# Giving one batch's softplus, half-splitting and transpose copies first place on their engines

## The chip, the cores and the metric

The kernel runs on one core of a Trainium2 chip. The metric is the time of the whole program on the device, in microseconds, as the median of several runs. The core has five engines that work side by side, each through a list of instructions of its own: TensorE (PE, matmuls; the loading of their weights is listed apart as PEld), VectorE (DVE), ScalarE (ACT), GpSimd (POOL) and SyncE (SP), which here issues the DMA transfers.

## The reference: what is computed

```python
def sm_attn(qq, kk, vv):                       # per batch and head
    s = scale * np.matmul(qq, kk.transpose(0, 1, 3, 2))
    s = s - np.max(s, axis=-1, keepdims=True)
    a = np.exp(s)
    a = a / (np.sum(a, axis=-1, keepdims=True) + 1e-09)
    return np.matmul(a, vv)
p_packed = sm_attn(p, k, v)                    # 32 packed queries look at 576 tokens
out = sm_attn(q, p_packed, p_packed)           # 576 tokens look at the 32 packed rows
...
x = out.transpose(0, 2, 1, 3).reshape(B * S, H * D)
h = x @ w_in
g = np.maximum(h, 0.0) + np.log1p(np.exp(-np.abs(h)))      # softplus
return g @ w_out
```

There are 8 batches of 576 tokens, 8 heads of 64, and a feed-forward part of 512 to 2048 to 512. q, k, v and p are float32; w_in and w_out arrive as 64-bit floats, and the kernel turns them into 32-bit ones itself.

## The kernel before: how the work is staged

**Algebra.** For one batch the second attention gives weights `aT` (packed rows by tokens, in two groups of four heads) that multiply `p_packed`. The kernel never forms `out`: it multiplies `p_packed` by `w_in` first (`make_m`, result `m`), and then `h = m^T @ aT`. Products that need more precision than one pass gives are made from a high and a low half of both sides, three matmuls instead of four: `at_h`/`at_l` (lines 525 and 526), `mh`/`ml` (558 and 559), `gh`/`gl` (594 and 595), `wo_h`/`wo_l` (238 and 244). The high half is a copy on ACT (or DVE for `gh`), the low half is the difference, made on DVE.

**Units.** After the attention of batch 0, the main loop goes through 128 units, a unit being one batch b and one block f of 128 columns of the 2048. Unit (b, f) has `gemm1` (line 580: twelve matmuls into two banks `ph` of 288 tokens), then softplus: ACT takes the absolute value of both banks (602), the exponential (604) and the logarithm (605), DVE then takes the maximum with 0 of `ph` and adds (607), which is the last reader of the banks. Two banks `ph` exist, so the next unit's `gemm1` waits for this. For batch 0 the exponential and the logarithm go over all 576 tokens at once, in other batches bank by bank. POOL sets the last 64 tokens aside (611), DVE splits the others into `gh` and `gl`. Two units later `gemm2` (618) multiplies them by `wo_h` and `wo_l`: four blocks of tokens, three matmuls each, accumulated over f in four banks `acc`. Units 0 and 1 of batch 0 have no `gemm2` beside them yet.

**Between the units.** At unit u, `make_m` for unit u + 2 is issued when a new group of columns begins. In batch 0 such a group has 256 columns, so that it comes at every second unit; in the others it has 512. It takes two banks out of the pool `ps_m`, which has two, and the same two banks serve each small product of the attention of the next batch, which is spread in steps between the blocks of `gemm2`.

**Turned q and k.** For batches 0 and 1, `transposed` (lines 254 to 269) turns q and k by matmuls with an identity into a bank (262), and ACT copies the bank to SBUF (268, `T_k` and `T_q`). For later batches DVE turns them (254). During batch 0's units the attention of batch 1 runs, so its sixteen copies `T_k` and `T_q` fall there; those of batch 0 come before the first unit.

**Conversion of the weights.** `convert` is a generator over 32 tiles, sixteen of w_in and sixteen of w_out, in the order i0 i1 o0 o1 i2 i3 o2 o3 and so on. One tile takes a load by SP (156), two steps of ACT (200 and 204, which make `m` and `r`), two of DVE (206 and 211) and one addition of POOL (219), which writes `w_in_sb` directly or, for w_out, a tile `t` from which ACT makes `wo_h` and DVE `wo_l`. Two to four staging tiles take turns: from the seventeenth tile on there are two. The steps begin in the attention of batch 0 and go on through its units, 1.6 steps after each block of `gemm2`. A tile of w_in is needed by `make_m`, a tile of w_out by `gemm2`.

**What sets the order.** PE's instructions stand in the order in which the text issues them (`manual_schedule` for PE alone). Those of the other engines are ordered when the program is built: of the operations that are ready by the builder's own reckoning, the one with the highest priority is taken, and without further word the one issued earlier in the text has the higher one. `tc.high_priority(offset=FRONT)`, FRONT being 1000, moves what is issued inside it ahead by that much. In the kernel before, the steps of batch 0's attention, `make_m(0, 0)` and `weights(0)` stand in it. On the chip each engine goes through its list in the order thus fixed.

Of the kernel before, what the change touches and what calls it, by code (L numbers as in the profile page):

```python
# [2 lines left out]

# [23 lines left out]
def pack_attention_then_softplus_ffn(  # L27
# [10 lines left out]
    nc = tc.nc  # L38
# [7 lines left out]
    C = S // 2  # L46
# [40 lines left out]
    def bank(nm):  # L87
        if spare:
            spare.append(spare.pop(0))
            pool, tag = spare[-1]  # L90
            return pool.tile([P, 512], F32, tag=tag, name=nm)
        return ps_m.tile([P, 512], F32, tag="m", name=nm)
# [164 lines left out]
    def transposed(nm, b, g, hh):  # L257

        src = loaded[nm, b, g]
        ps = bank(f"psT_{nm}_{b}_{g}_{hh}")  # L260
        for i in range(HS):
            nc.tensor.transpose(
                ps[:, i * NP:(i + 1) * NP],
                src[:, hh, 2 * i:2 * i + 2, :].rearrange("x s d -> x (s d)"),
                ident[:NP, :NP],
            )
        dst = work.tile([P, C], F32, tag="T", name=f"T_{nm}_{b}_{g}_{hh}", bufs=4)
        nc.scalar.copy(dst, ps[:, :C])  # L268
        return dst

    def scores(nm, b, g, c, lhs, rhs):
# [259 lines left out]
    def m_cols(b):  # L531

        return MC if b else MC // 2

    def make_m(b, c, res):


        n = m_cols(b)
        pss = [bank(f"psm_{b}_{c}_{g}") for g in range(G)]
        for g, ps in enumerate(pss):  # L540
            for hh in range(HG):
                o = D * g
                nc.tensor.matmul(  # L543
                    ps[hh * J:(hh + 1) * J, :n],
                    res["pt"][g][o:o + D, hh * J:(hh + 1) * J],
                    w_in_sb[o:o + D, hh, c * n:(c + 1) * n],
                    start=True, stop=True,
                )
        pool, th, tl = (cv, "t", "r") if b and c % 2 == 0 else (work, "mh", "ml")
        halves = []  # L550
        for g, ps in enumerate(pss):
            o = g * n % MC
            if o == 0:
                mh = pool.tile([P, MC], F32R, tag=th, name=f"mh_{b}_{c}_{g}", bufs=2)
                ml = pool.tile([P, MC], F32R, tag=tl, name=f"ml_{b}_{c}_{g}", bufs=2)
                halves.append((mh, ml))
            cols = slice(o, o + n)
            nc.scalar.copy(mh[:, cols], ps[:, :n])  # L558
            nc.vector.tensor_tensor(  # L559
                ml[:, cols], ps[:, :n], mh[:, cols].bitcast(F32), op=ALU.subtract  # L560
            )
        res["m"][c] = halves
# [112 lines left out]
    FRONT = 1000  # L675
# [15 lines left out]
    res = [{"pt": [], "aT": {}, "m": {}} for _ in range(B)]  # L691
# [24 lines left out]
    ahead, chain, due = iter(()), iter(()), 0.0  # L716
    for u in range(len(units) + LAG):
        if u < len(units):
            b, f = units[u]
            if f == 0:  # L720
                if (b + 1) % BG == 0 and b + 1 < B:
                    pack_transposed((b + 1) // BG, pt)
                ahead = attention(b + 1) if b + 1 < B else iter(())
                due = 0.0
            chain = softplus(b, f, gemm1(b, f, res[b]), gs)
            next(chain)
            if f == NF - 1:
                if (b + 2) % BG == 0 and b + 2 < B:
                    pt = load_pack((b + 2) // BG, (nc.sync,))
                for _ in ahead:  # L730
                    pass
                if b + 1 < B:
                    weights(b + 1)
        if u >= LAG:
            b2, f2 = units[u - LAG]
            gh, gl = gs.pop((b2, f2))
            if f2 == 0:
                acc = [ps_acc.tile([P, DM], F32, tag="acc", name=f"acc_{b2}_{t}") for t in range(NT)]
        last = u >= LAG and f2 == NF - 1 and b2 % 2 == 1
        if last:  # L740
            both = rests(b2)
            next(both)
        for t in range(NT):
            if u >= LAG:
                gemm2_tile(
                    acc[t], gh, gl, f2, slice(t * P, (t + 1) * P), f2 == 0, f2 == NF - 1
                )
                if f2 == NF - 1:
                    store(acc[t], [(0, b2, t * P, P)], f"{b2}_{t}", t)
            if u < len(units):  # L750
                due += PACE if b != FIRST - 1 else PACE_FIRST
                while due >= 1:
                    next(ahead, None)
                    due -= 1
                if b == 0:
                    cdue += CONV
                    while cdue >= 1:
                        next(conv, None)
                        cdue -= 1
            next(chain, None)  # L760
        if last:
            next(both)
        if u + 2 < len(units):


            nb, c = units[u + 2][0], units[u + 2][1] * P
            if c % m_cols(nb) == 0:
                make_m(nb, c // m_cols(nb), res[nb])


# [27 lines left out]
```

## Time and profile before

| | us |
|---|---|
| median of 3 runs | 775.51 |
| lowest and highest of them | 773.61 and 777.2 |
| the profiled execution | 774.48 |
| its span, first to last instruction | 772.7 |

The profile is of one execution, taken by the hardware profiler. Times are microseconds from the start of the span. A row of the timeline has start, length, engine, line of the kernel, operation, output and inputs, and in brackets how long the engine was idle before it and which operation ended this. A row of the waits has the waiting engine and line, the one it waited for, and the sum, the number and the longest of the waits. A row by stretch has the stretch, its length, the busy time of PE, PEld, DVE, ACT and POOL with the number of instructions, the granted clock of PE as a share of full speed, the share of the DMA engines and GB/s. Over the whole span PE is busy 94%, DVE 68%, ACT 56% and POOL 13%.

### The profile page before, as it was taken

How to read it: one execution, taken by the hardware profiler on the slowest of the kernel's cores; microseconds unless marked ns; L12 is line 12 of the kernel's file. 1: busy time of each engine (PE TensorE's matmuls, PEld its weight loads, DVE VectorE, ACT ScalarE, POOL GpSimd, SP SyncE). 2: the span in 40 equal slices, each digit the busy share in tenths (PEclk: the TensorE clock that was granted, in tenths of full speed). 3: DMA queues.
4: the chain of work that ended last, by engine and by line, in shares of the span. 5: the costliest groups of instructions: out<-in, count | busy, mean ns of one | idle time of the engine just before them, and what ended most of it. 6: DMA issues, size and time to landing. Idle time of an engine off the chain costs nothing.

```text
span 772.7 us, 14153 instructions
## 1 busy us (share of the span) xinstructions
PE 729.3 (94%) x5360; PEld 577.0 (75%) x5360; DVE 527.4 (68%) x1092; ACT 435.3 (56%) x1057; POOL 99.0 (13%) x166
## 2 busy tenths in 40 slices
PE   6457997999999999999999999999999999999997
PEld 4346675687788778877887777878787777888886
DVE  2697869975877559575877559576877558565554
ACT  5667977666455445565555455565555355555540
POOL 1253434200000000000010000000010000000110
PEclk9969999999999999999999999999999999999999
DMA  9977644534302342052402332043401400010002
GB/s 205 247 194 179 180 133 125 120 74 78 76 17 68 63 68 57 1 116 47 87 0 69 62 63 62 1 98 51 92 1 55 75 2 1 1 55 1 1 1 68
DMA packets 149668, 55.97 MB, mean 72 GB/s; under 512 B 116320, under 2 KB 142944, under 8 KB 149600
## 3 DMA queue, kind: packets, MB, share of 16 engines
q1 hardware_dynamic: 149328, 55.00, 31.9%
q8 instruction: 42, 0.69, 0.4%
q14 instruction: 26, 0.21, 0.1%
q10 hardware_dynamic: 272, 0.07, 0.0%
HBM read 45.61 MB, written 9.44 MB: 71 GB/s over the span
## 4 chain that ended last, share of the span: by engine, by line
PE 82%; DVE 6%; ACT 6%; DMA 4%; POOL 1%; issue 1%; SPq 0%; ACTq 0%; DVEq 0%; POOLq 0%
PE acc L618 41%; PE ph L580 26%; PE acc_m L618 6%; PE psm L543 4%; PE ps L275 2%; DMA w_in_sb<-in_q 2%; PE psp L318 1%; PE psa L308 1%; DMA k<-in_k 1%; ACT m L200 1%; DVE at_l L526 1%; DVE t L211 1%; POOL t L219 1%; ACT e L604 1%; DVE t L206 1%
## 5 line engine op out<-in xcount | busy, mean ns | idle before, releaser
L602 ACT ACTIVATE e<-ph 128x288 f32<-128x288 f32 x256 | 103.1, 404 | 189.3 <-PE ph L580 142.4
L618 PE MATMUL acc<-wo_h,gh 128*128 128x512 f32 x512 | 207.6, 405 | 0.0
L607 DVE SCALAR_TENSOR_TENSOR e<-ph,e 128x288 f32<-128x288 f32 x256 | 113.3, 451 | 131.9 <-ACT e L605 128.2
L618 PE MATMUL acc<-wo_l,gh 128*128 128x512 f32 x512 | 200.9, 392 | 0.0
L618 PE MATMUL acc<-wo_h,gl 128*128 128x512 f32 x512 | 200.8, 392 | 0.0
L580 PE MATMUL ph<-at_h,mh 128*128 128x288 f32 x512 | 158.9, 310 | 14.8 <-ACT at_h L525 7.5
L580 PE MATMUL ph<-at_l,mh 128*128 128x288 f32 x512 | 153.3, 299 | 3.7 <-DVE at_l L526 3.7
L580 PE MATMUL ph<-at_h,ml 128*128 128x288 f32 x512 | 152.7, 298 | 0.0
L580 PEld LDWEIGHTS ph<-at_h,mh 128*128 128x128 f32 x512 | 97.6, 191 | 48.8 <-DVE e L607 10.8
L611 POOL COPY rest<-e 128x64 f32<-128x64 f32 x128 | 53.2, 416 | 575.8 <-DVE e L607 544.2
L618 PEld LDWEIGHTS acc<-wo_h,gh 128*128 128x128 f32 x512 | 96.2, 188 | 27.4 <-issue 10.2
L618 PEld LDWEIGHTS acc<-wo_h,gl 128*128 128x128 f32 x512 | 96.1, 188 | 21.0
L604 ACT ACTIVATE e<-e 128x288 f32<-128x288 f32 (+1 forms) x240 | 109.5, 456 | 3.9
L605 ACT ACTIVATE e<-e 128x288 f32<-128x288 f32 (+1 forms) x240 | 109.4, 456 | 3.2
L618 PEld LDWEIGHTS acc<-wo_l,gh 128*128 128x128 f32 x512 | 96.4, 188 | 13.0
L580 PEld LDWEIGHTS ph<-at_l,mh 128*128 128x128 f32 x512 | 97.8, 191 | 8.2 <-DVE at_l L526 5.3
L580 PEld LDWEIGHTS ph<-at_h,ml 128*128 128x128 f32 x512 | 97.8, 191 | 0.0
L595 DVE TENSOR_TENSOR gl<-e,gh 128x512 fp32r<-128x512 f32 x128 | 87.7, 685 | 5.5
L558 ACT CAST mh<-psm 128x512 fp32r<-128x512 f32 (+1 forms) x72 | 35.9, 540 | 53.5 <-PE psm L543 53.4
L594 DVE CAST gh<-e 128x512 fp32r<-128x512 f32 x128 | 55.5, 434 | 5.1
L559 DVE TENSOR_TENSOR ml<-psm,mh 128x512 fp32r<-128x512 f32 (+1 forms) x72 | 42.8, 623 | 20.2 <-ACT mh L558 19.6
L543 PE MATMUL psm<-w_in_sb,pt 64*32 64x512 f32 (+1 forms) x576 | 40.0, 560 | 9.7 <-ACT T_k L268 4.8
(79 smaller groups left out, 693.5 us busy)
## 6 DMA issues: line engine op xcount, KB each, us to landing
v<-in_v SPq DMA_DIRECT2D x16, 576.0 KB, 5.0
x_i<-in_moe_w_in SPq DMA_DIRECT2D x28, 256.0 KB, 4.5
k<-in_k SPq DMA_DIRECT2D x48, 144.0 KB, 3.1
q<-in_q SPq DMA_DIRECT2D x48, 144.0 KB, 3.2
x_o<-in_moe_w_out SPq DMA_DIRECT2D x11, 512.0 KB, 3.8
out<-o SPq DMA_DIRECT2D x18, 256.0 KB, 2.5
rest<-in_moe_w_out SPq DMA_DIRECT2D x5, 512.0 KB, 6.0
k<-in_k SPq DMA_DIRECT2D x4, 576.0 KB, 6.5
```

The lines of the kernel that those rows point to most:

```text
L543: nc.tensor.matmul(ps[hh * J:(hh + 1) * J, :n], res["pt"][g][o:o + D, hh * J:(hh + 1) * J], w_in_sb[o:o + D, hh, c * n:(c + 1) * n], start ...
L558: nc.scalar.copy(mh[:, cols], ps[:, :n])
L559: nc.vector.tensor_tensor(ml[:, cols], ps[:, :n], mh[:, cols].bitcast(F32), op=ALU.subtract)
L580: nc.tensor.matmul(ph[:, :C], x[:, ms], y[:, g, cs], start=(i == 0), stop=(i == 3 * G - 1),)
L594: nc.vector.tensor_copy(hi, x)
L595: nc.vector.tensor_tensor(lo, x, hi.bitcast(F32), op=ALU.subtract)
L602: nc.scalar.activation(es[c], hv[c], AF.Abs)
L604: nc.scalar.activation(x, x, AF.Exp, scale=-1.0)
L605: nc.scalar.activation(x, x, AF.Ln, bias=1.0)
L607: nc.vector.scalar_tensor_tensor(es[c], hv[c], 0.0, es[c], op0=ALU.max, op1=ALU.add)
L611: nc.gpsimd.tensor_copy(rest[:, rest_at(b, f), r:r + REST], e[:, NT * P:])
L618: nc.tensor.matmul(acc, x[:, cs], y[:, f, :], start=(first and i == 0), stop=(last and i == 2),)
```

## The change

Three things are put inside `tc.high_priority(offset=FRONT)`: the copy of each turned q and k (batches 0 and 1; those of batch 0 stand inside one already), the first step of softplus of batch 0 (absolute value, exponential, logarithm, maximum and addition, but not the later steps, the copy of the rest and the split), and every `make_m` of batch 0 after the first. For other batches `nullcontext()` leaves things as they were. The set of operations, their sizes, tiles and buffers stay the same.

```diff
-from contextlib import ExitStack
+from contextlib import ExitStack, nullcontext
...
         dst = work.tile([P, C], F32, tag="T", name=f"T_{nm}_{b}_{g}_{hh}", bufs=4)
-        nc.scalar.copy(dst, ps[:, :C])
+        with tc.high_priority(offset=FRONT):
+            nc.scalar.copy(dst, ps[:, :C])
         return dst
...
             chain = softplus(b, f, gemm1(b, f, res[b]), gs)
-            next(chain)
+            with tc.high_priority(offset=FRONT) if b == 0 else nullcontext():
+                next(chain)
             if f == NF - 1:
...
             nb, c = units[u + 2][0], units[u + 2][1] * P
             if c % m_cols(nb) == 0:
-                make_m(nb, c // m_cols(nb), res[nb])
+                with tc.high_priority(offset=FRONT) if nb == 0 else nullcontext():
+                    make_m(nb, c // m_cols(nb), res[nb])
```

## The prediction

> **What bounds the kernel now.** I read the page first, for where TensorE (PE) is not full.
>
> ```profile
> span 772.7 us, 14153 instructions
> PE   6457997999999999999999999999999999999997
> ```
>
> A digit is 19.3 us. From the eighth digit on PE is full, and no edit of this change acts after batch 0 and attention 1, so what it can win lies before about 150 us. There I asked for one stretch, from the end of unit 0's first matmuls to just after unit 14's first wait, and for PE's waits in it, grouped.
>
> ```profile
> 46.90:143.00 96.10, 78.83 (x635) 58.91 (x635) 78.43 (x159) 75.35 (x158) 41.61 (x38) 0.95 0.61 157
> PE ph L580 <- DVE e L607: 7.2, 4, 3.0
> PE psm L543 <- ACT T_k L268: 4.8, 2, 4.5
> PE psm L543 <- ACT T_q L268: 2.5, 2, 1.7
> PE psm L543 <- POOL w_in_sb L219: 1.7, 1, 1.7
> PE psm L543 <- ACT a1T L309: 0.7, 1, 0.7
> PE psa L308 <- DVE ml L559: 0.3, 1, 0.3
> ```
>
> The first row gives the length and then the busy time of PE, weight loads, DVE, ACT, POOL. PE is idle 96.10 - 78.83 = 17.3 us, DVE 17.7, ACT 20.8: no engine is full, so it is latency and order that bound this stretch. The other rows say by whom PE was held (us, times, longest): 7.2 + 4.8 + 2.5 = 14.5 us of the 17.3 end with an operation that the change moves to the front: the max-and-add of softplus that frees a bank of ph, and the copies of turned k and q that free the banks psm needs. The last three rows, 2.7 us, end elsewhere. The timeline of PE gives the single stalls (start, length of the matmul or group, idle before it):
>
> ```profile
> 51.49 1.07 PE L543 MATMUL psm<-w_in_sb,pt 64*32 64x256 f32 x8 [4.55 <-ACT T_k L268]
> ...
> 60.64 0.61 PE L580 MATMUL ph<-at_h,mh 128*128 128x288 f32 x1 [3.05 <-DVE e L607]
> ...
> 75.37 0.40 PE L580 MATMUL ph<-at_h,mh 128*128 128x288 f32 x1 [1.84 <-DVE e L607]
> ...
> 121.34 0.67 PE L543 MATMUL psm<-w_in_sb,pt 64*32 64x256 f32 x16 [1.71 <-ACT T_q L268]
> ...
> 128.82 0.40 PE L580 MATMUL ph<-at_h,mh 128*128 128x288 f32 x1 [1.68 <-DVE e L607]
> ...
> 136.25 0.67 PE L543 MATMUL psm<-w_in_sb,pt 64*32 64x256 f32 x16 [1.66 <-POOL w_in_sb L219]
> ```
>
> **The change, part by part.** No instruction is added or removed and PE keeps its written order. The order of ACT, DVE, POOL and SP is set when the program is built: among operations that the builder thinks ready, the one with the higher priority is placed first. So each price below is the time of what stood in front.
>
> *The copies of turned k.* ACT's timeline after unit 0:
>
> ```profile
> 46.56 0.68 ACT L604 ACTIVATE e<-e 128x576 f32<-128x576 f32 x1
> ...
> 48.46 0.62 ACT L238 CAST wo_h<-t 128x512 fp32r<-128x512 f32 x1 [0.66 <-POOL t L219]
> 49.86 0.62 ACT L238 CAST wo_h<-t 128x512 fp32r<-128x512 f32 x1 [0.79 <-POOL t L219]
> 50.39 0.68 ACT L605 ACTIVATE e<-e 128x576 f32<-128x576 f32 x1
> 50.97 0.38 ACT L268 COPY T_k<-psT_k 128x288 f32<-128x288 f32 x1
> ```
>
> Between exponential and logarithm stand conversions of the weights, two of which wait for POOL. With them behind, the logarithm starts at about 46.56 + 0.6 = 47.2, the first copy at 47.8 and ends at 48.1, where now it ends at about 51.4. That is 3.3 us, and the 0.25 that is left of the 4.8 (the second bank) goes in part: I take 3.5. The logarithm too is 3.2 us earlier, so the max-and-add is done before PE wants the bank.
>
> *Softplus.* After unit 1:
>
> ```profile
> 57.72 0.70 ACT L604 ACTIVATE e<-e 128x576 f32<-128x576 f32 x1
> 58.30 0.66 ACT L200 ACTIVATE m<-x_o 128x512 f32<-128x512 f32 x1
> 58.85 0.68 ACT L605 ACTIVATE e<-e 128x576 f32<-128x576 f32 x1
> L607 DVE SCALAR_TENSOR_TENSOR e<-ph,e 128x288 f32<-128x288 f32 x256 | 113.3, 451 | 131.9 <-ACT e L605 128.2
> ```
>
> One conversion, 0.55 us from start to start, stands between the two. From the logarithm's end, 59.5, to PE's start at 60.64 are 1.1 us, of which one max-and-add (last row, 451 ns each) needs 0.45: some 0.6 is other work ahead on DVE. So of this stall about 0.55 + 0.6, rounded up to 1.4 with the conversion work ahead of the exponential, can go; the rest, 1.6 us, stays, because unit 1 has no second product to cover it. After unit 12 it is more:
>
> ```profile
> 125.00 0.69 ACT L604 ACTIVATE e<-e 128x576 f32<-128x576 f32 x1
> ...
> 127.23 0.68 ACT L605 ACTIVATE e<-e 128x576 f32<-128x576 f32 x1
> ```
>
> From 125.00 to 127.23 are 2.2 us where 0.6 do: three conversion steps lie between, 1.6 us, nearly the whole stall of 1.68. The stall of 1.84 at 75.37 I price the same way at 1.7. What is left of the 7.2, 0.6, goes with them. Sum for softplus: 1.4 + 1.7 + 1.6 + 0.6 = 5.3.
>
> *The copies of turned q.*
>
> ```profile
> 120.28 0.62 ACT L238 CAST wo_h<-t 128x512 fp32r<-128x512 f32 x1 [1.27 <-POOL t L219]
> 120.80 0.39 ACT L268 COPY T_q<-psT_q 128x288 f32<-128x288 f32 x1
> ```
>
> The copy stood behind a conversion that waited 1.27 us for POOL and took 0.52: together 1.8, the stall of 1.71. With the other one, 2.5 - 1.7 = 0.8, that is 2.5. The copies in attention 0 had priority already and now have more: they may pass another step of the same attention, one operation of ACT, so -0.6 to +0.6; I take 0, as nothing in it changes length.
>
> *The halves.* No stall of PE ends with mh, and ml ends one of 0.3. Gain 0.3 at most; and at worst each of the fourteen ml that remain, about as long as a max-and-add, puts 0.45 us in front of something on DVE that sets the end, 6 us. I take 0, nearest to the 0.3: the half is wanted a unit later, and what it passes are mostly conversion steps, which go into the rival below.
>
> *The clock.* Granted clock is the third number from the end here; the first after the length is PE's busy time.
>
> ```profile
> 46.60:50.00 3.40, 0.35 (x3) 0.14 (x1) 2.76 (x4) 1.95 (x4) 2.96 (x2) 0.98 0.34 101
> 50.00:53.40 3.40, 1.63 (x16) 0.43 (x16) 3.28 (x8) 3.40 (x8) 2.24 (x2) 0.52 1.04 283
> 53.40:56.80 3.40, 3.40 (x20) 2.95 (x13) 3.33 (x6) 2.18 (x5) 1.60 (x1) 0.50 1.09 250
> 56.80:60.20 3.40, 0.79 (x8) 0.59 (x6) 1.25 (x4) 3.07 (x7) 1.26 (x1) 0.98 1.12 217
> 60.20:63.60 3.40, 2.96 (x12) 2.96 (x13) 3.40 (x7) 1.16 (x3) 1.92 (x2) 0.52 1.10 266
> 60.64 3.25 PE ph L580 x12
> 101.30 1.61 PE ph L580 x12
> ```
>
> The first five rows of the fence above are stretches of 3.4 us, the last two come from the chain of waits (start, length). In such steps the clock follows how busy PE was in the step before: 0.35 and 0.79 us busy, and 1.63 too, are followed by half speed, 3.40 by full speed. Unit 2's twelve matmuls took 3.25 us in the slow step, unit 8's 1.61 in a fast one; unit 1's lay in a slow step too. If the two stalls shrink to 1.2 and 1.6 us, PE is busy some 2 us in each step, which lies between what brought half speed (1.63) and what I have seen bring full speed. So the gain is 0 to 3.3; I take 1.6.
>
> The Trainium skill, "TensorE: Matmul & The Clock Gate", Part 1, says that PE's clock is halved after an idle window of about 3.4 us, and that such windows run freely. The rows agree on the step, but show a halving after a step that was nearly half busy. By that rule neither shortened stall could halve the clock, and the sum below would be 1.7 us larger.
>
> *Sum and what holds it back.* 3.5 + 5.3 + 2.5 + 0 + 1.6 = 12.9 us. Not all of it can come. First, DVE's 78.43 us of work stay; in 96.1 - 12.9 = 83.2 us it would be 94% busy against 82% now, with its waits of the same kind. Second, the conversion of the weights is just in time where the stretch ends. POOL finishes each tile:
>
> ```profile
> 54.12 1.60 POOL L219 TENSOR_TENSOR w_in_sb<-t,r 128x512 int32<-128x512 int32 x1 [1.36 <-DVE t L211]
> ...
> 134.92 1.27 POOL L219 TENSOR_TENSOR w_in_sb<-t,r 128x512 int32<-128x512 int32 x1
> 67.73 0.66 PE L543 MATMUL psm<-w_in_sb,pt 64*32 64x256 f32 x16
> 111.78 3.88 DMA x_o<-in_moe_w_out
> 67.41 0.69 ACT L200 ACTIVATE m<-x_i 128x512 f32<-128x512 f32 x1
> ```
>
> The tile that ends at 55.7 is used at 67.73, 12 us later; the last one ends at 136.2 and is used at 136.25. In between twenty tiles take 80.5 us, 4.0 each. Every microsecond that PE gains ahead of this must be gained by the conversion too. It can gain: its first step after 55 us stands at 67.41 on ACT, behind operations that follow PE, so it slides forward with PE. But with two staging tiles a tile cannot take less than half of its load and its two ACT steps, (3.88 + 1.3) / 2 = 2.6 us, and conversions now stand behind everything. I take half of the sum, 6.5 us: then DVE is 78.43 / 89.6 = 88% busy and conversion needs (80.5 - 6.5) / 20 = 3.7 us a tile, between 2.6 and 4.0. The profiled execution took 774.48 us (span 772.7 and 1.8 around it), so 768.0 for it; the median of the runs shown, 775.51, is 1.0 above it, so **769.0**. This forecast holds from 765.5 to 771.5. A measurement of this kernel tells about 0.5%, 3.9 us, from no change.
>
> **The rivals.** *All of it:* conversions run into the gaps that the freed ACT leaves (20.8 us idle) and DVE fills up: 775.5 - 12.9 = 762.6. For it speaks that conversion steps ran or waited in front in each of the stalls whose ACT rows stand above; against it DVE at 94%.
>
> *Nothing:* the stalls of the middle vanish and come back as one at the last tile of w_in: PE arrives 12 us early at the matmul that now starts at 136.25 and waits for a tile that still lands at 136.2: 775.5. The lead that melts from 12 us to none speaks for it; against it, that the steps of conversion were ordered behind PE's results and not behind their loads. The change could also do nothing of what it says, where the builder thought the conversion step ready long before the favoured one: then it still places it first. That gives the same 775.5. Wo_h's waits for POOL show that its view of time differs from the chip's, yet at 125.00 and 57.72 the favoured step was plainly next.
>
> *Slower:* conversion starves. Fourteen units are left after the first; if in each the favoured steps push the conversion by one more step of 0.6 us on ACT or DVE, the last tile lands 8 us later, at 144.3, PE waits there, and each microsecond past 136.2 costs one. Its next load goes out only after its own ACT step, so the delay passes into the 3.88 us load. Half of that, 4 to 5 us, is the likelier size: 780. It decides from the point where the last tile lands later than 136.3. The Trainium skill, same page, Part 1, "Architectural detail", says ACT and DVE execute strictly in order, so that a favoured step which has to wait also holds the conversions behind it; no run so far shows a favoured step that does so; the row at 120.28, a conversion whose wait for POOL held up a favoured copy, is the same rule from the other side. For this rival speaks that there was no slack at the end; against it, that it needs ACT, 78% busy, or DVE to have no room.
>
> **How the numbers follow.** Forecast 0.47, all of it 0.13, nothing 0.24, slower 0.16. Faster by more than 3.9 us: 0.47 + 0.13 = 0.60; within it 0.24; slower 0.16. The range leaves out a little of the full gain and the deep end of the starving: 762.0 to 779.5.
>
> **What would show it.** Right: the 4.55 and both T_q stalls gone, ACT's rows L604 and L605 back to back in batch 0, unit 2's matmuls in less than 3.25 us, the matmul now at 136.25 starting near 130. Wrong: a wait for w_in_sb of more than 5 us there, or a wait for wo_l; DVE still 82% busy in the shortened stretch; or the same order of ACT as before. If PE's idle time in the stretch falls by less than 3 us, the reasoning on order was wrong; if it falls by 10 or more, the holding back was.

## The result, and the profile after

| | before, same occasion | after |
|---|---|---|
| median, us | 774.78 (4 runs, 773.61 to 777.2) | 786.09 (4 runs, 784.1 to 788.37) |
| ratio, 95% interval | | 1.0141 [1.0122, 1.016] |
| span of the profiled execution, us | 772.7 | 782.3 |
| mean granted clock of it | 0.985 | 0.976 |

The change makes the kernel 1.4% slower, 11.3 us. Lines of the changed kernel stand one to three higher: 268 is 269, 543 is 544, 558 and 559 are 559 and 560, 580 is 581, 602 to 607 are 603 to 608.

From the page of the changed kernel, PE's row and that of its granted clock, with the span cut in 40 slices of 19.6 us:

```profile
PE   6559898699999999999999999999999999999997
PEclk9859898999999999999999999999999999999999
```

The fourth slice is fuller than before, 9 for 7, but the fifth is 8 for 9 and the eighth 6 for 9, and the clock's digits dip in the fifth and the seventh; from the ninth on nothing differs. So the loss lies where the gain was looked for. The two stretches from the first matmul of unit 0 to the first of batch 1, before:

```profile
38.71:153.28 114.57, 94.20 (x719) 70.35 (x719) 96.48 (x188) 86.26 (x177) 46.69 (x43) 0.92 0.62 156
```

and after, with the shorter stretch that answers to the one of 96.10 us in the prediction:

```profile
37.67:162.70 125.03, 100.92 (x718) 75.35 (x719) 100.88 (x190) 86.89 (x177) 44.37 (x43) 0.86 0.56 143
45.86:152.80 106.94, 85.91 (x635) 64.03 (x635) 84.77 (x165) 76.74 (x159) 40.87 (x40) 0.88 0.56 143
```

The same work takes 125.03 us in place of 114.57, 10.5 more; unit 0 started 1.0 us earlier, so batch 1 starts 9.4 later, and the span is 9.6 longer. PE is idle 24.1 us in place of 20.4, which is 3.7 of the 10.5. The rest is in PE's busy time, 100.92 against 94.20 for the same matmuls, and the granted clock in these rows is 0.86 against 0.92. PE's waits in the shorter stretch, grouped:

```profile
PE psm L544 <- POOL w_in_sb L219: 8.6, 2, 5.5
PE psm L544 <- ACT T_k L269: 4.3, 2, 3.9
PE ph L581 <- DVE e L608: 3.1, 3, 2.0
PE psp L319 <- ACT a1T L310: 2.6, 1, 2.6
PE psm L544 <- ACT a1T L310: 0.9, 1, 0.9
PE ps L276 <- ACT T_k L269: 0.9, 1, 0.9
PE psm L544 <- ACT T_q L269: 0.5, 1, 0.5
```

The waits that end with a favoured operation fell from 14.5 us to 8.8 (4.3 + 3.1 + 0.9 + 0.5). In their place stand operations that were not favoured: the last addition of the conversion of w_in, 8.6 us where it was 1.7, and the copy `a1T` of batch 1's attention, 3.5 where it was 0.7. The single stalls in PE's timeline:

```profile
49.89 1.29 PE L544 MATMUL psm<-w_in_sb,pt 64*32 64x256 f32 x16 [3.90 <-ACT T_k L269]
57.27 0.40 PE L581 MATMUL ph<-at_h,mh 128*128 128x288 f32 x1 [1.96 <-DVE e L608]
...
86.83 0.87 PE L319 MATMUL psp<-v,a1T 96*32 96x64 f32 x24 [2.63 <-ACT a1T L310]
...
124.60 1.11 PE L544 MATMUL psm<-w_in_sb,pt 64*32 64x256 f32 x16 [3.06 <-POOL w_in_sb L219]
...
144.59 1.11 PE L544 MATMUL psm<-w_in_sb,pt 64*32 64x256 f32 x16 [5.49 <-POOL w_in_sb L219]
```

Set beside the starts of the units (first matmul of each, from PE's timelines), they show an early gain that is lost again in three places:

| start, us | u0 | u2 | u4 | u7 | u10 | u13 | u14 | batch 1 |
|---|---|---|---|---|---|---|---|---|
| before | 38.7 | 60.6 | 75.4 | 95.8 | 114.6 | 136.8 | 142.1 | 153.3 |
| after | 37.7 | 57.3 | 70.0 | 97.3 | 116.5 | 145.6 | 151.9 | 162.7 |

At unit 4 the changed kernel is 5.4 us ahead, as was hoped. By unit 7 it is 1.5 behind (the stall at 86.83 and what follows), and between units 10 and 13 it loses another 6.9 (the two waits for w_in_sb and a slow stretch after the first).

The first of these losses is not yet a late tile: up to 92.5 us POOL finishes the tiles of the conversion about when it did before (the addition at 92.48 stood at 92.81). There PE's lead runs into the attention of batch 1. PE comes to that product (319) at 83.66, 4.1 us earlier than before (87.80), but the copy `a1T` that its second half needs starts at 86.31, only 1.4 us earlier than before (87.70).

**How the last tile of w_in comes late.** ACT's timeline of the changed kernel around one staging tile of w_out, `x_o`:

```profile
129.46 0.67 ACT L200 ACTIVATE m<-x_o 128x512 f32<-128x512 f32 x1
130.03 0.67 ACT L605 ACTIVATE e<-e 128x576 f32<-128x576 f32 x1
130.69 0.40 ACT L269 COPY T_q<-psT_q 128x288 f32<-128x288 f32 x1
130.98 0.69 ACT L606 ACTIVATE e<-e 128x576 f32<-128x576 f32 x1
132.39 0.40 ACT L269 COPY T_q<-psT_q 128x288 f32<-128x288 f32 x1 [0.72 <-PE psT_q L262]
132.68 0.67 ACT L204 ACTIVATE r<-x_o 128x512 int32<-128x512 uint32 x1
...
138.08 0.68 ACT L200 ACTIVATE m<-x_i 128x512 f32<-128x512 f32 x1 [0.75 <-DMA x_i<-in_moe_w_in]
```

The same two steps in the kernel before:

```profile
122.89 0.66 ACT L200 ACTIVATE m<-x_o 128x512 f32<-128x512 f32 x1
123.45 0.66 ACT L204 ACTIVATE r<-x_o 128x512 int32<-128x512 uint32 x1
```

Two steps read a staging tile, `m` and `r`. Before, they are neighbours. After, four favoured steps and a wait for PE come between them, and the tile is held for 3.9 us in place of 1.2. SP's queue then issues the load of the last tile of w_in into it at 133.38 (before at 124.14), and ACT now waits for that load. Of these 9.2 us the gap between the two readings makes 2.7. The other 6.6 were there when `m` began, and had built up over the tiles before: the addition of POOL that came at 99.62 now comes at 103.46, the one at 115.95 at 122.97, the one at 118.96 at 127.32. DVE and POOL after that:

```profile
138.26 0.81 DVE L608 SCALAR_TENSOR_TENSOR e<-ph,e 128x288 f32<-128x288 f32 x2
138.99 0.83 DVE L344 STREAM_TRANSPOSE a<-ps 128x288 f32<-128x288 f32 x2
...
141.31 0.75 DVE L353 TENSOR_TENSOR a<-a,m 128x576 f32<-128x576 f32 x1
141.98 0.42 DVE L206 TENSOR_SCALAR t<-m 128x512 int32<-128x512 int32 x1
```

```profile
53.70 1.32 POOL L219 TENSOR_TENSOR w_in_sb<-t,r 128x512 int32<-128x512 int32 x1 [2.29 <-DVE t L211]
...
143.27 1.27 POOL L219 TENSOR_TENSOR w_in_sb<-t,r 128x512 int32<-128x512 int32 x1 [3.83 <-DVE t L211]
```

`m` is done at 138.76, but DVE's first step on it starts only at 141.98 (before, 0.13 us after it). Only the first 0.3 us of this are a favoured step, L608; the others are steps of batch 1's attention and the splitting into `gh` and `gl`, which the change does not favour. The last addition ends at 144.54 and PE goes on at 144.59. From the tile that ends at 55.0 the twenty tiles take 89.5 us, 4.5 each, where before they took 4.0.

### The profile page after: what moved, and what is told of

It is laid out like the page before. It is cut to its first block, busy times and chain, and to the rows that moved or that the text cites. A ratio compares the mean times of both kernels' runs of the same rounds, so it can differ in the third digit from the quotient of the medians.

```text
span 782.3 us, 14149 instructions
## 1 busy us (share of the span) xinstructions
PE 736.4 (94%) x5360; PEld 582.1 (74%) x5360; DVE 530.4 (68%) x1092; ACT 435.7 (56%) x1057; POOL 96.4 (12%) x166
## 4 chain that ended last, share of the span: by engine, by line
PE 83%; DVE 7%; ACT 5%; DMA 2%; POOL 1%; issue 1%; SPq 1%; ACTq 0%; POOLq 0%; DVEq 0%
PE acc L619 41%; PE ph L581 25%; PE acc_m L619 6%; PE psm L544 4%; PE ps L276 2%; DMA w_in_sb<-in_q 2%; PE psp L319 2%; PE psa L309 1%; DVE at_l L527 1%; ACT e L605 1%; DVE t L211 1%; DVE e L608 1%; POOL t L219 1%; ACT e L603 1%; DVE t L206 1%
## 5 line engine op out<-in xcount | busy, mean ns | idle before, releaser
L608 DVE SCALAR_TENSOR_TENSOR e<-ph,e 128x288 f32<-128x288 f32 x256 | 113.1, 452 | 138.9 <-ACT e L606 135.7
L581 PEld LDWEIGHTS ph<-at_h,mh 128*128 128x128 f32 x512 | 98.5, 192 | 44.5 <-DVE gl L596 9.4
L612 POOL COPY rest<-e 128x64 f32<-128x64 f32 x128 | 51.3, 401 | 576.2 <-DVE e L608 549.4
L596 DVE TENSOR_TENSOR gl<-e,gh 128x512 fp32r<-128x512 f32 x128 | 91.1, 712 | 5.7
L559 ACT CAST mh<-psm 128x512 fp32r<-128x512 f32 (+1 forms) x72 | 35.9, 540 | 57.5 <-PE psm L544 57.3
```

What stands on the lines that cost most here:

```text
L581: nc.tensor.matmul(ph[:, :C], x[:, ms], y[:, g, cs], start=(i == 0), stop=(i == 3 * G - 1),)
L596: nc.vector.tensor_tensor(lo, x, hi.bitcast(F32), op=ALU.subtract)
L608: nc.vector.scalar_tensor_tensor(es[c], hv[c], 0.0, es[c], op0=ALU.max, op1=ALU.add)
L612: nc.gpsimd.tensor_copy(rest[:, rest_at(b, f), r:r + REST], e[:, NT * P:])
```

## The experiments

My theory after the result: the conversion of the weights and the favoured operations want the same slots on ACT and DVE, and conversion has no time to spare; what the favoured ones win, PE pays at w_in_sb and by stalls that bunch. Rivals: one of the three edits does the harm by itself; the loss is the clock's; only one engine's conversion steps matter; or conversion has nothing to do with it and the new order among the favoured operations and the attention is worse in itself. Every median stands beside one of the kernel before from the same occasion.

### The three edits one at a time

Each kernel has one hunk of the diff: `t_only` the copies of turned q and k, `s_only` softplus, `m_only` make_m.

> Only the copies of turned q and k are put in front. Theory (starved conversion): what delays the conversion of the weights is mainly softplus in front, so the copies alone take out most of the 4.8 + 2.5 us of PE's waits for T_k and T_q and push few conversion steps: 769 to 774 us against about 775, and no wait for w_in_sb above 2.5 us. Rival (a favoured copy that waits for PE holds up what is behind it on ACT): the copies carry the loss, 780 to 787 us, with conversion steps late behind them.

> Only the first step of softplus of batch 0 is put in front. Theory (starved conversion): this is the part with most work, six operations in each unit, so it carries most of the slowdown: 781 to 787 us, with waits of PE for w_in_sb of over 4 us in sum and the last tile of w_in finished after 140 us. Rival: softplus in front takes away the 7.2 us of waits for the max-and-add and costs nothing: 768 to 774 us.

> Only the halves of p_packed @ w_in of batch 0 are put in front. Both theories: fourteen small pairs that were wanted a unit later change little, 773 to 778 us. A third possibility, that the halves on DVE are what pushes the conversion's two DVE steps back: over 780 us.

| | median, us | ratio to before (775.08) |
|---|---|---|
| copies alone | 778.67 | 1.0035 [1.0016, 1.0054] |
| softplus alone | 782.56 | 1.0096 [1.0074, 1.0117] |
| make_m alone | 776.55 | 1.0022 [1.0006, 1.0039] |

Each edit alone is slower, softplus most, and the three together make 1.5%, about the whole. None wins what the prediction gave it.

The copies alone were expected to win, and the theory does not cover their loss: the last tile of w_in ends at 137.1, 0.9 later than before, and PE does not wait for w_in_sb at all. In the profile (780.75 us, the slowest of ten) it takes 120.6 us from the first unit to batch 1, 6.0 more than before, though PE's idle time is 20.8 us against 20.4. What grew is PE's busy time, 99.8 from 94.2, at a granted clock of 0.87 against 0.92.

With softplus alone the last tile of w_in, in POOL's timeline, is late too:

```profile
139.88 1.32 POOL L219 TENSOR_TENSOR w_in_sb<-t,r 128x512 int32<-128x512 int32 x1 [1.44 <-DVE t L211]
```

It ends at 141.2, 5.0 later than before, and PE waits for it once, 2.8 us, where over 4 were expected. From the first unit to batch 1 that kernel takes 120.6 us and PE is idle 20.2 of them, no more than before (20.4): its stalls are not longer in sum, they lie elsewhere, and its matmuls take longer, at a granted clock of 0.86.

### Without the conversion

The staging, the conversion steps and their loads are taken out of both kernels, and the weights' tiles are filled with a constant; the attention, softplus and all matmuls stay.

```diff
-    conv = convert(order)
+    fill = w_in_sb[:, :, :DFF - G * SI * D]
+    nc.gpsimd.memset(fill, 0.01)
...
+    conv = iter([None] * (NF * 16))
```

> The kernel before without the conversion of the weights: no loads of w_in and w_out, none of the conversion's steps on ACT, DVE and POOL; w_in_sb, wo_h and wo_l are filled with a constant at the start, so the output is another. Theory (conversion steps in front of urgent work cause the stalls of before): in batch 0 the waits for T_k, T_q and the max-and-add all but vanish except where two units have no second product, PE's idle time after unit 0 falls from 17 us to under 6, and the time is 755 to 764 us. Rival (the stalls come from the attention of batch 1 itself): it keeps most of the 17 us, above 768 us.

> The changed kernel without the conversion of the weights, as in the run beside it. Theory (the change loses because it starves the conversion): with nothing to starve it is equal to noconv_before within 0.4% or up to 3 us faster. Rival (the favoured operations hold up the attention of batch 1 or wait for PE in front of other work): it stays slower than noconv_before by 5 us or more.

Medians 760.16 for the kernel before and 760.11 for the changed one, ratios to the whole kernel before (774.5) 0.9806 [0.9782, 0.983] and 0.9801 [0.9773, 0.9829]. PE's waits from 46.9 to 143 us, first without and then with the change:

```profile
PE ph L580 <- DVE e L607: 2.7, 2, 2.2
...
```

```profile
PE ph L581 <- DVE e L608: 2.7, 2, 2.0
```

Without conversion the favoured order wins nothing and costs nothing that these intervals, about 2 us to each side, can tell. The waits for T_k, T_q, w_in_sb and a1T are gone from both. So without conversion there is no loss, and of the stalls that the change aims at 2.7 us are left. (Its ACT, DVE and POOL work and its loads go together here, so this run does not say which of them counts.)

### Conversion in front too, or its tiles earlier

`conv_front` is the changed kernel with each step of the conversion that is issued among the units favoured as well, loads included; `win_ahead` loads and converts each pair of w_in tiles one pair of w_out earlier.

```diff
-                        next(conv, None)
+                        with tc.high_priority(offset=FRONT):
+                            next(conv, None)
```

```diff
+    order += [("i", 0), ("i", 1)]
...
-        if f % 2 == 0:
-            order += [("i", f), ("i", f + 1)]
+        if f % 2 == 0 and f + 2 < NF:
+            order += [("i", f + 2), ("i", f + 3)]
```

> The whole change, and the conversion steps issued among the units are put in front as well, so that they stand against the favoured operations in the order of the text again, and all of it stands ahead of the attention of batch 1. Theory (starved conversion): the waits for w_in_sb (8.6 us) and the half-speed clock after them go, 770 to 777 us, at or below the kernel before. Rival (the loss comes from favoured operations waiting for PE on ACT, or from the attention of batch 1 held back): 782 us or more, as the attention is then held back further.

> The changed kernel with the order of the tiles altered: each pair of w_in tiles is converted one pair of w_out tiles earlier; the number of steps stays. Theory: the waits of 3.1 and 5.5 us for w_in_sb go, and with them the half-speed stretches behind them (about 3 and 1.7 us), so 776 to 780 us; the waits shift to wo only if w_out is now late. Rival (the late w_in tile is only where a general lack of room on DVE shows): the same loss turns up at another wait, 783 us or more.

`conv_front`: 781.85, ratio 1.0095 [1.0077, 1.0114], far from the 770 to 777 of the theory and just short of the rival's 782. The last tile is there early, at 130.0, and PE's waits from 45 to 155 us have changed their place once more:

```profile
PE ph L581 <- DVE e L608: 7.2, 4, 3.8
PE psm L544 <- ACT T_k L269: 5.9, 2, 4.5
PE psm L544 <- ACT a1T L310: 2.3, 1, 2.3
PE psa L309 <- ACT a L285: 1.9, 1, 1.9
```

No wait for w_in_sb is left, but the stalls at softplus and T_k are back at their size of before or above it, and the attention of batch 1, which is not favoured, is late by itself (a1T, a). `win_ahead`: 780.68 against 774.5, 1.0063 [1.0038, 1.0089]. Its waits for w_in_sb are gone as well; what takes their place, in PE's waits from 45 to 153 us, is a load of k:

```profile
PE psT_k L262 <- DMA k<-in_k: 6.2, 1, 6.2
```

SP's queue shows why (start and length of an issue):

```profile
42.33 1.26 SPq L156 DMA_DIRECT2D rest<-in_moe_w_in  x2
43.69 0.55 SPq L127 DMA_DIRECT2D k<-in_k  x1
```

The load of k goes out behind those of w_in that were moved ahead of it, at 43.69; in the kernel before it went out at 36.77. So the waits for w_in_sb can be removed, and 0.95% or 0.63% of the 1.41% stay: tiles in time are not enough, and the waits that grew instead are those of work displaced for them. The kernel before was not run with these two protections, so what they cost by themselves is not known.

### One engine's conversion steps

In the changed kernel, only ACT's two steps of each tile are favoured (`act_steps_front`), or only DVE's two (`dve_steps_front`), by `with tc.high_priority(offset=FRONT):` around them. `after_conv20` leaves priorities alone and issues conversion steps faster, CONV 2.0 for 1.6.

> The changed kernel, and of the conversion only its two reading steps on ACT (m and r) are put in front as well. Theory (favoured operations come between these two steps, so a staging tile is given back late, its next load goes out late and the last w_in tile lands at 144.5 instead of 136.2): the tiles come earlier again, the waits for w_in_sb fall from 8.6 us to under 3, 777 to 781 us. Rival (the two DVE steps of the conversion are what is late): no better than 784.

> The changed kernel, and of the conversion only its two steps on DVE are put in front as well. Theory of the run beside this one (ACT's reading steps and the staging tiles are what is late): no better than 783 us, waits for w_in_sb over 5 us. Rival (DVE is what is late): 776 to 781 us, those waits under 3 us.

> The changed kernel with 2.0 instead of 1.6 conversion steps issued after each block: they stand earlier in the text, so before more of the attention of batch 1, and still behind the favoured operations. Theory (the conversion loses against the favoured operations, not against the attention): little changes, 783 to 788 us. Rival (it is short against everything): w_in is no longer late, 775 to 780 us.

| | median, us | ratio to before (775.32) |
|---|---|---|
| ACT's steps favoured | 776.91 | 1.0022 [1.001, 1.0034] |
| DVE's steps favoured | 778.61 | 1.0042 [1.0027, 1.0058] |
| CONV 2.0 | 786.03 | 1.0136 [1.0115, 1.0156] |

Either engine's steps alone give back most of the loss: each against the kernel before of its occasion, 1.6 and 3.3 us of 11.3 are left. With ACT's steps in front the last tile of w_in ends at 137.0. The expectation that DVE's steps alone would not help, 783 us or more, was wrong; with them the last tile ends at 139.5 and PE waits 2.4 us for it. Issuing the steps earlier in the text changes nothing that can be told; the last waits for w_in_sb are the same 8.6 us as in the changed kernel.

### Softplus with ACT's steps; all steps from the start

`s_act` has the softplus hunk alone and ACT's conversion steps in front; `act_dve` is the changed kernel with both engines' steps in front.

> Softplus of batch 0 in front (as in s_only) and the conversion's two reading steps on ACT in front, nothing else. Theory (softplus in front pays nothing by itself and loses only by delaying the conversion): s_only's 7 us are given back, 773 to 777 us. Rival (softplus in front delays the attention of batch 1 too): 779 us or more.

> The changed kernel with both pairs of conversion steps, those on ACT and those on DVE, in front. Theory (the conversion is all that was starved): at or below the better of the two single ones, 773 to 777 us. Rival (then the attention of batch 1 is what is starved, as in conv_front): 779 to 783 us.

`s_act`: 782.27 against 775.28, 1.0089 [1.0064, 1.0114], no better than softplus alone, where 773 to 777 was expected. PE's timeline shows that its loss lies in another place, about unit 0:

```profile
46.24 0.61 PE L582 MATMUL ph<-at_h,mh 128*128 128x288 f32 x1 [3.60 <-ACT at_h L527]
...
55.10 1.20 PE L264 MATMUL psT_k<-ident,k 96*128 96x96 f32 x6 [3.69 <-DMA k<-in_k]
```

Unit 1 begins at 61.45, where in the kernel before it began at 53.9. From there to batch 1 this kernel takes 100.4 us, softplus alone 106.1, and the kernel before 99.4: from unit 1 on the protection works, and the loss has moved ahead of it. In `s_act` the conversion steps are in front during batch 0's attention too; but so they are in `act_steps_front`, where unit 1 begins at 53.7, so this alone does not explain the late start, and its cause stays open. `act_dve`: 778.39, 1.004 [1.0026, 1.0054], between its two expectations. Unit 1 begins at 59.0, and from it to batch 1 are 98.5 us. The next runs start the protection only with the units.

### Conversion in front from the first unit on, with and without the change

A flag that is set when the attention of batch 0 has been issued favours ACT's and DVE's conversion steps from there on. `late_front` is the changed kernel with it, `before_late_front` the kernel before.

```diff
-            nc.scalar.activation(m, hi.bitcast(F32), AF.Copy, scale=2.0**-112)
+            with tc.high_priority(offset=FRONT) if front else nullcontext():
+                nc.scalar.activation(m, hi.bitcast(F32), AF.Copy, scale=2.0**-112)
...
+    front.append(True)
```

> The changed kernel, and the conversion's two steps on ACT and two on DVE are put in front as well, but only those issued from the first unit on. Theory (starved conversion is the whole loss): the start is as in the changed kernel, units 1 to 16 take about 98 to 100 us instead of 111.6, 772 to 776 us. Rival (something else of the change costs too): 778 us or more.

> The kernel before with the same conversion steps in front from the first unit on, without the change. Theory (the favoured operations of the change bring nothing of themselves, as without a conversion): the same as late_front within 0.4%. Rival (once the conversion is safe the change pays): late_front is 4 us or more faster than this.

| | median, us | ratio to before (775.14) |
|---|---|---|
| change and conversion in front | 776.77 | 1.0022 [1.001, 1.0034] |
| conversion in front alone | 777.38 | 1.0031 [1.0021, 1.0042] |

Of the 1.41% that the change costs, 0.22% are left, 1.6 us of 11.3. That is close to the 772 to 776 of the theory, though the way there is not as expected: in the profile (778.70 us, 1.9 above the median) unit 1 to batch 1 takes 104.2 us and not 98 to 100. The kernel before loses 2.2 us by the same protection, so what is left goes with the protection. And with conversion protected the change itself makes no difference that these intervals tell. PE's waits from 45 to 155 us, with the change and then without:

```profile
PE ph L589 <- DVE e L616: 7.6, 4, 3.2
PE psm L552 <- ACT T_k L277: 4.5, 1, 4.5
```

```profile
PE ph L588 <- DVE e L615: 7.6, 5, 3.2
PE psm L551 <- ACT T_k L276: 6.2, 1, 6.2
```

The stalls that the change was to remove are there at about their size of before, 7.2 and 4.8. That fits the theory that the favoured operations gain from the very slots that a timely conversion needs.

### Is it the clock?

By the records, the 10.5 us that the units of batch 0 lost are 3.7 of idle time, 6.3 of lost clock (in steps of half a microsecond, PE's busy time times one minus the granted clock, summed: 13.0 against 6.6) and 0.4 of other. Four kernels tried whether this second part can be moved by itself. `keep_busy` is the changed kernel with 16 more matmuls ahead of each make_m from the seventh on, to fill the waits for w_in; `busy_early` is the kernel before with 30 and 12 more behind units 0 and 1. `trip1` and `trip4` are the kernel before with one or four round trips between PE and ACT at 20 places in the later batches, where nothing else waits.

```diff
+        if b == 0 and c >= 6:
+            mh, at_h = res["m"][c - 1][0][0], res["at"][0]
+            for _ in range(16):
+                nc.tensor.matmul(
+                    pss[0][:, :C], mh[:, :P], at_h[:, 0, :C], start=True, stop=True
+                )
```

```diff
+        if u < LAG:
+            junk = ps_acc.tile([P, DM], F32, tag="acc", name=f"junk_{u}")
+            for _ in range((30, 12)[u]):
+                nc.tensor.matmul(
...
```

```diff
+        if u < len(units) and 2 <= b <= 6 and f in (5, 7, 9, 11):
+            for i in range(4):
+                ps = bank(f"trip_{u}_{i}")
+                nc.tensor.matmul(ps[:, :P], ident, ident, start=True, stop=True)
+                with tc.high_priority(offset=FRONT):
+                    nc.scalar.copy(ident, ps[:, :P])
+            ps = bank(f"trip_{u}_end")
+            nc.tensor.matmul(ps[:, :P], ident, ident, start=True, stop=True)
```

The last of these is `trip4`; in `trip1` the loop is `range(1)`.

> The changed kernel with sixteen extra matmuls (128x128 by 128x288, about 2.1 us at full speed) ahead of make_m for the last two groups of columns, into the bank that make_m then overwrites; they need nothing that is late and run inside the waits of 3.1 and 5.5 us for w_in_sb. Theory (a good part of the loss is PE's clock, halved after a 3.4 us step with about 2 us of idle time or more): the half-speed stretches at 124 to 131 us shrink or go, 782 to 785 us, although work was added. Rival (the clock matters little): no gain, or up to 2 us slower, 786 to 788 us.

> The kernel before, with 30 and 12 extra matmuls (128x128 by 128x288) on PE after units 0 and 1, into a free bank that nobody reads; they fill the idle times of 4.6 and 3.1 us there. Theory (idle time of about 1.8 us or more in one step of 3.4 us halves the clock): the clock stays at full speed from about 47 us on where it is now half until 64 us, units 1 and 2 take about 1.6 us each instead of 3.2, and the time falls by 2 to 4 us, 771 to 773 us, although work is added. Rival (the clock does not matter, since ACT and DVE set the pace there): 774 to 777 us.

> The kernel before, and at twenty places in batches 2 to 6, where PE is full, PE multiplies the identity with itself, ACT copies the result back and PE's next matmul waits for this: one round trip, some 0.8 us of idle time of PE at each place. Both theories: about 20 x 1 us slower, 790 to 800 us, clock at full speed.

> As the run beside it, with four round trips one behind the other at each of the twenty places, some 3 us of idle time. Theory (idle time of about 2 us or more within a step of 3.4 us brings half speed for one step or more): besides four times the loss of one trip come half-speed steps at most places, 1 to 2 us each, so the loss is over five times that of one trip and the mean granted clock falls by 0.04 or more. Rival (the clock is not set off by this): four times the loss, clock as in the run beside it.

| | median, us | ratio to before |
|---|---|---|
| change, PE kept busy | 785.4 (before 774.5) | 1.013 [1.0104, 1.0156] |
| before, PE kept busy early | 776.06 (before 775.32) | 1.0013 [0.9998, 1.0028] |
| one trip at 20 places | 797.35 (before 775.28) | 1.0281 [1.0252, 1.0311] |
| four trips at 20 places | 857.64 (before 775.28) | 1.1063 [1.1028, 1.1098] |

In `keep_busy` the clock did stay up where the changed kernel had lost it at the first wait for w_in_sb:

```profile
125.10:128.50 3.40, 2.67 (x19) 2.35 (x17) 3.40 (x8) 2.55 (x5) 1.70 (x2) 1.00 0.43 154
```

From unit 10 to batch 1 it took 44.0 us against 46.2, but it had lost more than that before, at the second wait the clock fell all the same, and its time is not told apart from the changed kernel's. In `busy_early` the clock was full for one step more and then fell again, and nothing was won.

The round trips cost 22.1 / 20 = 1.1 us and 82.4 / 20 = 4.1 us a place, 3.7 times as much for four as for one, where the theory had said over five times. The clock fell behind 6 of the 20 places of `trip4` and behind none of `trip1`. This lets equal stretches of one execution be compared. Here are two of `trip4`, each from the place in block 9 to the one in block 11, with the same matmuls (74 or 75 by the records), first of batch 2 and then of batch 3:

```profile
310.79:325.83 15.04, 13.62 (x74) 10.74 (x75) 8.78 (x17) 6.75 (x18) 0.73 (x2) 0.89 0.00 1
410.50:423.98 13.48, 12.06 (x75) 9.20 (x75) 8.95 (x17) 6.63 (x18) 0.92 (x2) 1.00 0.00 1
```

Where the clock fell the stretch takes 15.04 us, and in the other four batches 13.47 or 13.48. From block 7 to block 9 it is the other way round: batch 2 keeps its clock and takes 13.14 us, the other four lose it and take 14.64 to 14.70. So where PE is full, one fall to half speed costs about 1.5 us by itself.

For batch 0 this gives a reason to take the 6.3 us of lost clock seriously, above all with the copies alone and with softplus alone, whose idle time did not grow. But PE also waits for ACT and DVE there, and neither `keep_busy` nor `busy_early` won time where the clock stayed up. As a cause of their own in these units the 6.3 us stay open.

## Why the prediction was wrong

**What bounds it** held: the stretch, the stalls and that PE is bound there by latency and order. The loss too lies in it, but for a few tenths.

**The copies of k**, 3.5 us: wrong. T_k's waits went from 4.8 to 5.2 us (4.3 + 0.9). The logarithm did move ahead, to 1.1 us behind the exponential (45.52 and 46.66), but the copy did not. I reckoned that the copy would pass the two conversions `wo_h` that wait for POOL. ACT's timeline of the changed kernel:

```profile
47.43 0.62 ACT L238 CAST wo_h<-t 128x512 fp32r<-128x512 f32 x1
48.83 0.62 ACT L238 CAST wo_h<-t 128x512 fp32r<-128x512 f32 x1 [0.79 <-POOL t L219]
49.36 0.69 ACT L269 COPY T_k<-psT_k 128x288 f32<-128x288 f32 x2
```

It still stands behind both. That fits the rival I gave for "nothing", that the builder thinks the conversion ready long before the copy and so places it first; the builder's own times are not in a trace, so this is argued, not shown.

**Softplus**, 5.3, and **the copies of q**, 2.5: right on their own stalls. The waits for the max-and-add fell from 7.2 to 3.1, those for T_q from 2.5 to 0.5, together 6.1 of the 7.8 I gave them. **The halves**: no stall ends with ml any more, as said; alone they cost 0.22%.

**The clock**, a gain of 1.6: right only at the start. Unit 2's twelve matmuls began at 57.27 and what followed them at 58.97, 1.70 us in place of 3.25. But over the stretch the sign was wrong, 6.3 us lost by the records, since I looked at the two slow steps that were there and not at those that new stalls would make. Two steps of the changed kernel, and the step that follows each:

```profile
82.80:86.20 3.40, 1.41 (x29) 0.79 (x27) 2.39 (x5) 2.84 (x5) 2.07 (x2) 1.00 0.36 136
86.20:89.60 3.40, 2.77 (x32) 2.60 (x33) 2.48 (x8) 0.58 (x3) 1.76 (x3) 0.50 0.75 186
120.30:123.70 3.40, 1.24 (x8) 0.66 (x6) 3.40 (x9) 3.18 (x6) 1.03 (x2) 1.00 0.32 128
123.80:127.20 3.40, 2.60 (x22) 1.79 (x23) 2.17 (x6) 0.65 (x2) 0.75 (x1) 0.50 0.69 178
```

The new stalls that end at 86.83 and 124.60 are each followed by a step at half speed (0.50); so is the one that ends at 144.59.

**The step that failed** is "Sum and what holds it back": "conversion needs (80.5 - 6.5) / 20 = 3.7 us a tile, between 2.6 and 4.0". It took 4.5. I had let conversion slide forward with PE and priced only its gain; but the steps that I moved ahead were moved ahead of conversion, and the upper bound of 4.0, which is what a tile took before, left out that it could become slower. One reading under it was wrong too: the row at 67.41 is the first step of the next tile of w_in, while ACT worked on tiles of w_out at 56.00 and 58.30, so conversion was not simply waiting behind PE. The rows of the staging tile show one of the places where it fell back: four favoured steps pass between its two readings, and its next load goes out late. That the loss comes from conversion standing behind the favoured steps is shown by two pairs of runs: without conversion, and with its four steps on ACT and DVE in front as well from the first unit on, the change makes no difference that the intervals tell, 0.1 and 0.6 us by the medians. The late last tile is not all of it. The 6.9 us lost between units 4 and 7 came before the tiles fell back, and the copies alone lose 3.6 us with the last tile only 0.9 later; there the rows show PE's lead running into batch 1's attention, and a lower clock.

**The rival "slower"** had the mechanism, the place and nearly the time: last tile at 144.3, measured 144.5, and a wait for w_in_sb of 5.49 us there, which was my sign for wrong. The case that no run had shown is there too: the favoured copy at 132.39 waits 0.72 us for PE, and a conversion step stands behind it. Its price was not right: I halved the 8 us to get 780, where the whole delay came, and a first wait of 3.06 and the slow steps behind the stalls came with it. That 144.3 was so near is partly luck: it was reckoned as 0.6 us in each of fourteen units, while the tiles were about level with before up to 92.5 us and fell back 8.4 us in the 35 us after that. Its chance of 0.16 was too small for what stood in my own text: no slack at the end, and every favoured operation put ahead of exactly this chain. The measured 786.09 lies 17.1 us above the forecast and 6.6 above the end of the range.

**The test on idle time**: PE's idle time in the stretch rose from 17.3 to 21.0 us, so the reasoning on order was wrong as a whole though right for single stalls. DVE became not fuller but emptier, 84.77 / 106.94 = 79% against 82%; the holding back that I put on DVE's fill did not come.

**Open**: how much of the loss the clock makes by itself; whether ACT's or DVE's conversion steps matter more, since either alone gives back most; what makes the copies alone slower, with hardly a late tile; and how protecting the conversion by itself costs the kernel before 2.2 us. A third staging tile, which would let loads run ahead, was not tried.

## What to carry to other kernels

Moving an operation ahead is paid by the operation whose slot it takes. Before favouring what PE waits for, list the background chains that share its engines (here staging tile, load, conversion, use), take from the trace how long before its use each result lands, and price the change by the chain with the least lead. If it has none at the end of the stretch, what the favoured order gains early comes back as waits, there or at the first other work that was not moved along, here the next batch's attention.

## What the runs showed of the hardware

Stalls well under 3.4 us were enough to halve the clock. In the rows above, 1.99 us without work in a step of 3.4 (82.80 to 86.20) were followed by half speed, though no single stall there was longer than 2.63 us; 2.16 us (120.30 to 123.70), with a longest stall of 3.06, as well. The Trainium skill, "TensorE: Matmul & The Clock Gate", Part 1, "HAM oscillation — how this bites in real kernels", gives the rule as no idle gaps above about 3.4 us; these two stalls stay below that and the clock fell, so here the measurement decides.

One step fell with less, in `busy_early`:

```profile
49.60:53.00 3.40, 2.33 (x25) 1.23 (x24) 3.28 (x8) 2.70 (x7) 2.06 (x2) 0.99 1.09 280
53.00:56.40 3.40, 2.33 (x11) 1.99 (x10) 2.79 (x4) 2.27 (x5) 2.22 (x2) 0.50 1.10 257
```

Only 1.07 us of the first step are idle. It holds many short matmuls; whether that is why stays open.

The record of the clock is not always right. In `act_dve` it reads 1.00 from 58.9 to 62.3, yet unit 1's matmuls start 0.24 us apart there, as they do in the half-speed steps of the kernel before; at full speed it is 0.13. So the start-to-start time of equal matmuls is worth a look beside the clock's column.

A small matmul that goes to ACT and back cost PE 22.1 / 20 = 1.1 us where it stood alone, its own matmuls included, and 82.4 / 80 = 1.0 in a row of four, falls of the clock included. Of the 1.1 the records name 0.4 as waiting time (7.9 us over the 20 places of `trip1`).
